# Seven block products in the order 1 5 6 2 7 3 4, with sums chained through PSUM pairs that ScalarE starts, and the last round's preparation one round later

## Chip, core and metric

One Trainium2 chip, one of its cores (core 0). The metric is the device time of one execution in microseconds. Before the change three runs took 802.03, 802.43 and 801.37 us, median 802.03.

The engines named below are TensorE (PE, with PEld for its weight loads), VectorE (DVE), ScalarE (ACT), GpSimd (POOL) and SyncE (SP). POOL and SP do almost nothing here but issue transfers: SP the loads, POOL the stores and the transfers that add to what lies at their target.

## The reference, cut to what matters

With x of 2048 rows (S) and 512 columns (D), weights of F = 1792 columns, all in fp32:

```python
# A: Fourier mixing, real part
a = x @ dft_hid_re.T
b = x @ dft_hid_im.T
A = dft_seq_re @ a - dft_seq_im @ b
# B: gated feed-forward
gate, up = x @ W_gate, x @ W_up
B = (gate * (gate > 0) * up) @ W_down
# mix, one gate value per row of x
g = sigmoid((x * gate_w).sum(-1, keepdims=True))
out = g * A + (1 - g) * B
```

## The kernel before

**Arithmetic.** Every fp32 operand is split into a high part and a low rest (a cast on ScalarE, then a subtraction on VectorE), and every product is three matmuls: high by low, low by high, high by high (`PARTS`, line 375). The large products are cut into 2 x 2 blocks and done with seven block products instead of eight. Which blocks are added to form the operands of product m stands in `LEFT` and `RIGHT` (lines 25 to 28); the tables are for the block stages, the rounds have their own sums in `Left.sum` (729) and `Sequence.rights` (874). Each matmul is 128 x 128 stationary by 512 columns moving, so a result is one PSUM bank (128 partitions x 512 fp32). There are eight banks. A `Pair` (339) is two banks.

**Stages in TensorE's order** (the letters are the names of the PSUM tiles in the profile):

- `c`: eight warm-up matmuls, then `Direct` (544, 96 matmuls, plain products for the first weight columns), then eleven `Block`s (491) of 84 matmuls. A Block is one (c, q): 256 columns of the gate and of the up weights by one half of the rows, as seven products of 12 matmuls, 6 into each bank of a pair (gate in one, up in the other). Weights of a new c are loaded and split by `w_prep` (458) while the block before runs.
- `a`: four `SpectralBlock`s (655), 84 matmuls each, for a and b.
- `c` again: two Blocks.
- `z`: two `Down` rounds (843, h @ W_down, 294 matmuls each) and four rounds with the sequence matrices, three `Sequence` (865) and the `Last` (904), 336 matmuls each. A round is seven products of 48 matmuls, in the order `ORDER_Z` (710). The left operands of the last two rounds were split earlier, stored, and are fetched back during the second of the four rounds (`Left.fetch`, 759, tensor `lb`).

**After a product.** The evacuations read the finished banks and combine them. In a Block (`evac`, 515) they work on one bank at a time: ScalarE copies or rectifies 512 wide, VectorE adds 512 wide from a bank and from SBUF (`t`, `u`). The sums that several products share are kept in SBUF. In a round (`Round.evac`, 811) `both` does the same bank by bank.

**PSUM.** A pool of eight tiles of one bank, handed out in turn; the first matmul into a bank overwrites (`start=True`). A Block takes six banks and the next one the two that are left, then those that are free again.

**The mix.** In the third and fourth rounds results are multiplied by the gate row and added to what earlier rounds stored in DRAM (`vd`, `zd`). For the Last round `prepare` (907) loads both, multiplies, adds and stores the sum back in `vd`, four pieces of 512 KB each from each of the two: eight loads, four stores, eight VectorE instructions 1024 wide. It is given `start + 150`, where start is the key at which the second round begins.

**Who sets the order.** Nothing is left to a scheduler of the language. Each step gets a key in units of one matmul (`op`), and `Plan` (129) lays out, once, when the program is built, an order for each engine, from a key, a due time and its own table of durations (`Step`, 90; `order`, 196). SBUF is 51 units of 4 KB per partition (`UNITS`); a step that begins a new buffer waits in the plan until a unit is free. On the chip each engine then runs its list in order, and waits where it must.

Lines that the change and the steps of the prediction touch: `ORDER`, `BANK` 29 and 30; `run` 262; `Weights` 414 and `w_prep` 458; `Block.evac` 515; `Spectral.prep` 646 and `SpectralBlock.evac` 680; `ORDER_Z` 710; `Round` 766, `evac` 811; `Sequence.rights` 874; `Last` 904 to 946; the keys from 960 to 1072.

Of the kernel before, what the change touches and what calls it, by code (L numbers as in the profile page):

```python
# [14 lines left out]
P = 128  # L15
# [9 lines left out]
LEFT = {1: ("11", "22", 1), 2: ("21", "22", 1), 3: ("11",), 4: ("22",), 5: ("11", "12", 1),  # L25
        6: ("21", "11", -1), 7: ("12", "22", -1)}
RIGHT = {1: ("11", "22", 1), 2: ("11",), 3: ("12", "22", -1), 4: ("21", "11", -1), 5: ("22",),
         6: ("11", "12", 1), 7: ("21", "22", 1)}
ORDER = (5, 2, 1, 3, 4, 6, 7)
BANK = {5: "a", 3: "a", 6: "a", 2: "b", 4: "b", 7: "b", 1: "c"}  # L30
# [98 lines left out]
class Plan:  # L129
# [30 lines left out]
    def read(self):  # L160
# [3 lines left out]
        seen, banks = {}, []  # L164
        for s in self.steps:
            for refs, writes in ((s.reads, False), (s.writes, True)):
                for r in refs:
# [7 lines left out]
                    if not r.base.uses and r.base.kind == "bank":  # L175
                        banks.append(r.base)
                    r.base.uses.append(s)

        for old, new in zip(banks, banks[8:]):
            new.uses[0].after.update(x for x in old.uses if x is not new.uses[0])  # L180
# [81 lines left out]
    def run(self, nc, unit, bank):  # L262
# [5 lines left out]
        for b in self.bufs:  # L268
            if b.uses and b.kind in ("unit", "bank"):
                first.setdefault(min(at[s] for s in b.uses), []).append(b)  # L270

        held, idle = [-1] * UNITS, [-9.0] * UNITS
        for n, s in enumerate(self.steps):
            for b in first.get(n, ()):
                if b.kind == "bank":
                    b.tile = bank(b)
                    continue
# [9 lines left out]
def kernel(ctx: ExitStack, tc, xP, xG, wf, wgu, wd, cr, ci, wri, gw, out):  # L287
# [19 lines left out]
    psum = ctx.enter_context(tc.tile_pool(name="psum", bufs=8, space=PSUM))  # L307
# [28 lines left out]
    def bank(b):  # L336
        return psum.tile([P, N], F32, name=b.name, tag="ps")

    class Pair:


        def __init__(self, name):
            self.name, self.banks = name, None

        def new(self):
            self.banks = [Buf(plan, self.name, [N], kind="bank") for _ in range(2)]

        def __getitem__(self, n):
            return self.banks[n].all
# [37 lines left out]
    def x_raw(q, m):  # L387

        a, *r = RIGHT[m]
        raw = piece[q, {6: "12", 7: "21"}[m] if m in (6, 7) else a] if not r or m in (6, 7) else buf(f"xs{m}")  # L390
        X[q, m] = buf(f"xh{m}", dtype=F32R), buf(f"xl{m}", dtype=F32R), raw

    def x_sum(q, m):
        a, *r = RIGHT[m]
        if r:
            combine(X[q, m][2].all, piece[q, a].all, piece[q, r[0]].all, r[1])
# [15 lines left out]
    SLOT = {5: 0, 1: 1, 2: 2, 4: 0, 3: 1, 7: 2, 6: 3}  # L412

    class Weights:
        def __init__(self, c):
            self.c = c
            self.raw = [buf(f"wr{i}", [4, 2, P]) for i in range(2)]
            self.sum = [buf(f"ws{i}", [3, 2, P]) for i in range(2)]
# [6 lines left out]
        def a_sum(self, i):  # L425
            r, o = self.raw[i], self.sum[i]
            E().vector.tensor_add(o[:, 0], r[:, 1], r[:, 2])
            E().vector.tensor_add(o[:, 1], r[:, 0], r[:, 1])
            E().vector.tensor_add(o[:, 2], r[:, 0], r[:, 3])
            E().scalar.copy(self.a[i][0].all, o.all)  # L430

        def a_lo(self, i):
            E().vector.tensor_sub(self.a[i][1].all, self.sum[i].all, f32(self.a[i][0].all))

        def b_sum(self, i):
            r = self.raw[i]
            E().vector.tensor_sub(r[:, 2:4], r[:, 2:4], r[:, 0:2])

        def b_hi(self, i):
            E().scalar.copy(self.b[i][0].all, self.raw[i].all)  # L440

        def b_lo(self, i):
            E().vector.tensor_sub(self.b[i][1].all, self.raw[i].all, f32(self.b[i][0].all))
# [11 lines left out]
        def of(self, m, i):  # L455
            return [t[:, SLOT[m]] for t in (self.a if m in (5, 1, 2) else self.b)[i]]
# [34 lines left out]
    class Block:  # L491


        def __init__(self, q, w):
            self.q, self.w = q, w
            self.t, self.g, self.u = buf("t"), buf("g"), buf("u")
            self.h = [buf(f"h{d}") for d in range(2)]
            self.ps = {k: Pair("c") for k in "abc"}
            for m in ORDER:
                for i in range(2):  # L500
                    pe(6, self.product, m, i)
                    self.evac(m, i, plan.now)
            h_out(q, w.c, self.h, plan.now + (8 if plan.now > 270 else 100))

        def product(self, m, i):
            w, x, ps = self.w.of(m, i), X[self.q, m], self.ps[BANK[m]]
            if m in (5, 2, 1) and i == 0:
                ps.new()
            n = 0
            for k in range(2):  # L510
                for a, b in PARTS:
                    mm(ps[i], w[a][:, k], x[b][:, k], start=m in (5, 2, 1) and n == 0, stop=n == 5)
                    n += 1

        def evac(self, m, i, key):
            a, b, c = (self.ps[k] for k in "abc")
            t, g, h = self.t, self.g, self.h

            def go():
                e = E()  # L520
                if m == 5:
                    e.scalar.copy(t[:, i], a[i])
                elif m == 2:
                    e.vector.tensor_add(t[:, i], t[:, i], b[i])
                elif m == 1:
                    e.vector.tensor_sub(t[:, i], c[i], t[:, i])

                elif m in (3, 4):
                    j, ps = (0, a) if m == 3 else (1, b)
                    if i == 0:  # L530
                        e.scalar.activation(g[:, j], ps[0], AF.Relu)
# [234 lines left out]
    class Round:  # L766
# [25 lines left out]
        def product(self, x, jj):  # L792
# [3 lines left out]
            if first:  # L796
                ps.new()
# [330 lines left out]
```

## Time and profile before

| what | value |
|---|---|
| median of three runs | 802.03 us (801.37 to 802.43) |
| span of the profiled execution, first to last instruction | 799.7 us |
| PE busy | 790.3 us, 99% of the span, 3464 matmuls |
| DVE busy | 665.6 us, 83% |
| ACT busy | 329.1 us, 41% |
| POOL busy | 91.7 us, 11% |
| moved by DMA | 192.79 MB, mean 241 GB/s |
| granted TensorE clock, mean | 0.999 |

The profile gives no device time of its own for the profiled execution; its span stands 2.3 us under the median, which is what lies around the span. All steps carry line 126, since a helper of the plan issues them; groups are told apart by the names of the tiles. `c`, `a` and `z` are PSUM tiles, `ch`/`cl` the high and low parts of a right operand of a round, `r` a loaded piece of a sequence matrix (from `cr` or `ci`), `lb` the stored left operands, `wr` raw weights, `ws` their sums. Matmuls are pipelined: each row lasts 0.39 us, and one starts about every 0.227 us.

### The profile page before, as it was taken

The numbers are of one execution on the slowest core, as the hardware profiler recorded it, in microseconds if no ns is written. First come the engines' busy times: TensorE is split into PE (matmuls) and PEld (weight loads), VectorE is DVE, ScalarE is ACT, GpSimd is POOL, SyncE is SP. The second block draws the span as 40 slices with busy tenths as digits, with TensorE's granted clock in tenths as the row PEclk, the third lists the DMA queues.
The fourth block names the chain that finished last, engine by engine and source line by source line (L and its number), as shares of the span: only waits on it lengthen the run. The fifth ranks groups of instructions, "written<-read, shape, count | busy, mean of one in ns | idle before, by whom it ended". The sixth has DMA issues, their size and how long they took to land.

```text
span 799.7 us, 9573 instructions
## 1 busy us (share of the span) xinstructions
PE 790.3 (99%) x3464; PEld 652.1 (82%) x3464; DVE 665.6 (83%) x791; ACT 329.1 (41%) x393; POOL 91.7 (11%) x146
## 2 busy tenths in 40 slices
PE   8999999999999999999999999999999999999997
PEld 7888888888888888888888888888888877888885
DVE  7999977868699466999985799996688849988995
ACT  5533221212133144275665668454334335434530
POOL 0101211111112122111131011001000100010000
PEclk9999999999999999999999999999999999999999
DMA  9514553232547599999899989118899995197424
GB/s 346 219 41 145 183 200 145 92 145 93 197 145 250 198 353 400 416 343 344 291 373 413 409 278 370 72 58 244 267 333 401 344 384 178 40 305 270 153 64 143
DMA packets 55039, 192.79 MB, mean 241 GB/s; under 512 B 6352, under 2 KB 6352, under 8 KB 54992
## 3 DMA queue, kind: packets, MB, share of 16 engines
q1 hardware_dynamic: 35120, 120.87, 41.6%
q0 software_dynamic: 19296, 70.26, 25.2%
q10 hardware_dynamic: 576, 1.05, 0.4%
q8 instruction: 27, 0.44, 0.2%
q14 instruction: 20, 0.16, 0.1%
HBM read 120.85 MB, written 71.31 MB: 240 GB/s over the span
## 4 chain that ended last, share of the span: by engine, by line
PE 91%; DMA 6%; DVE 2%; ACT 0%; issue 0%; SPq 0%; ACTq 0%; DVEq 0%
PE z L126 48%; PE c L126 34%; PE a L126 10%; DMA r<-ci 4%; DMA lb<-lb 1%; DVE cl L126 1%; DMA wf<-wf 1%; DVE r L126 0%; ACT ch L126 0%; DVE v L126 0%; DVE z L126 0%; ACT wf0h L126 0%; SPq L126 0%; ACTq L126 0%; DVEq L126 0%
## 5 line engine op out<-in xcount | busy, mean ns | idle before, releaser
L126 ACT CAST ch<-r 128x1024 fp32r<-128x1024 f32 x112 | 116.1, 1053 | 140.8 <-DVE r L126 54.6
L126 PE MATMUL z<-ch,ll 128*128 128x512 f32 x420 | 163.4, 389 | 0.0
L126 PE MATMUL z<-cl,lh 128*128 128x512 f32 x420 | 163.4, 389 | 0.0
L126 PE MATMUL z<-ch,lh 128*128 128x512 f32 x420 | 163.4, 389 | 0.0
L126 DVE TENSOR_TENSOR cl<-r,ch 128x1024 fp32r<-128x1024 f32 x112 | 134.6, 1221 | 27.4 <-ACT ch L126 20.5
L126 PE MATMUL z<-ch,lb 128*128 128x512 f32 x448 | 138.4, 389 | 0.7 <-ACT ch L126 0.7
L126 PEld LDWEIGHTS z<-ch,lb 128*128 128x128 f32 x448 | 84.1, 188 | 18.4 <-ACT ch L126 1.1
L126 PEld LDWEIGHTS z<-ch,lh 128*128 128x128 f32 x420 | 78.8, 188 | 16.5
L126 PEld LDWEIGHTS z<-ch,ll 128*128 128x128 f32 x420 | 78.8, 188 | 16.3
L126 PEld LDWEIGHTS z<-cl,lh 128*128 128x128 f32 x420 | 78.8, 188 | 16.3
L126 PE MATMUL z<-cl,lb 128*128 128x512 f32 x224 | 87.5, 391 | 1.4 <-DVE cl L126 1.3
L126 DVE TENSOR_TENSOR r<-r,r 128x1024 f32<-128x1024 f32 x64 | 76.5, 1219 | 3.6 <-DMA r<-ci 3.0
L126 DVE TENSOR_TENSOR cl<-hr,ch 128x1024 fp32r<-128x1024 f32 (+1 forms) x56 | 59.9, 1087 | 13.4 <-ACT ch L126 10.8
L126 ACT CAST ch<-hr 128x1024 fp32r<-128x1024 f32 (+1 forms) x56 | 51.3, 941 | 28.4 <-DMA hr<-hd 13.8
L126 PEld LDWEIGHTS z<-cl,lb 128*128 128x128 f32 x224 | 42.0, 188 | 11.3 <-DVE cl L126 2.6
L126 ACT ACTIVATE g<-c 128x512 f32<-128x512 f32 x26 | 15.5, 598 | 66.4 <-PE c L126 66.2
L126 PE MATMUL c<-xh,wb0l 128*128 128x512 f32 x104 | 40.5, 389 | 0.0
L126 PE MATMUL c<-xl,wb0h 128*128 128x512 f32 x104 | 40.5, 389 | 0.0
L126 PE MATMUL c<-xh,wb0h 128*128 128x512 f32 x104 | 40.5, 389 | 0.0
L126 PE MATMUL c<-xh,wb1l 128*128 128x512 f32 x104 | 40.5, 389 | 0.0
L126 PE MATMUL c<-xl,wb1h 128*128 128x512 f32 x104 | 40.5, 389 | 0.0
L126 PE MATMUL c<-xh,wb1h 128*128 128x512 f32 x104 | 40.5, 389 | 0.0
(191 smaller groups left out, 1321.3 us busy)
## 6 DMA issues: line engine op xcount, KB each, us to landing
hr<-hd SPq DMA_DIRECT2D x42, 512.0 KB, 7.4
r<-cr SPq DMA_DIRECT2D x32, 512.0 KB, 5.6
r<-ci SPq DMA_DIRECT2D x32, 512.0 KB, 9.2
hd<-hs POOLq DMA_DIRECT2D x28, 512.0 KB, 4.7
lb<-lb SPq DMA_DIRECT2D x28, 512.0 KB, 12.0
ad<-a POOLq DMA_DIRECT2D x16, 512.0 KB, 6.0
l<-ad SPq DMA_DIRECT2D x16, 512.0 KB, 8.8
wr<-wgu SPq DMA_DIRECT2D x14, 512.0 KB, 5.5
```

Source lines behind the costliest of these rows:

```text
L126: getattr(getattr(nc, self.engine), self.name)(*map(ap, self.a), **{k: ap(x) for k, x in self.k.items()})
```

## The change

- **Products.** All seven-product stages use one scheme in the order 1 5 6 2 7 3 4 (rounds: 1 5 6 3 7 2 4). `LEFT` and `RIGHT` give new operands; some are sums of a sum (product 6 of the right operand is block 22 minus the operand of 5). An x stage has four sums instead of five, and product 3 of the first half of the rows shares its split with `Direct`.
- **PSUM.** One tile of eight banks for the whole kernel, as four fixed pairs x, m, y, t. Only products 1 and 5 begin with `start=True`. ScalarE starts the others: after product 1 it copies pair x to pair y, and 6 and 7 accumulate there; after product 7 it copies y, negated, to t, and 4 accumulates there; 2 goes on in x and 3 in m. Pairs y and t are thus begun by ScalarE's write.
- **Evacuations** take both banks in one instruction, 1024 wide. In a Block ScalarE has four of 1024 and two of 512 (before: four of 512), VectorE two of 1024 and four of 512 (before: twelve of 512). In a round before the Last, ScalarE has six of 1024 (before: six of 512), VectorE two of 1024 (before: eight of 512 and one of 1024).
- **Weights.** The parts used by 1, 2, 4 need no sums; those for 5, 6, 7, 3 have four sums 256 wide, and are all prepared ahead of the block that uses them.
- **Keys.** `prepare` at `start + 540` with 40 between the pieces (before: `start + 150`, 24); refetch of the weights of c = 1 begins 140 ahead (before: 90); the `Last` round has no `ahead` step any more.

The diff, cut to its core:

```diff
-LEFT = {1: ("11", "22", 1), 2: ("21", "22", 1), 3: ("11",), 4: ("22",), 5: ("11", "12", 1),
-        6: ("21", "11", -1), 7: ("12", "22", -1)}
...
-ORDER = (5, 2, 1, 3, 4, 6, 7)
-BANK = {5: "a", 3: "a", 6: "a", 2: "b", 4: "b", 7: "b", 1: "c"}
+LEFT = {1: ("11",), 2: ("12",), 3: ("12", 6, -1), 4: ("22",), 5: ("21", "22", 1), 6: (5, "11", -1), 7: ("11", "21", -1)}
+RIGHT = {1: ("11",), 2: ("21",), 3: ("22",), 4: (6, "21", -1), 5: ("12", "11", -1), 6: ("22", 5, -1), 7: ("22", "12", -1)}
+ORDER = (1, 5, 6, 2, 7, 3, 4)
+BANK = {1: "x", 2: "x", 5: "m", 3: "m", 6: "y", 7: "y", 4: "t"}
+FIRST = (1, 5)
...
-    psum = ctx.enter_context(tc.tile_pool(name="psum", bufs=8, space=PSUM))
+    psum = ctx.enter_context(tc.tile_pool(name="psum", bufs=1, space=PSUM))
...
+    ps8 = Buf(plan, "ps", [8, N], kind="fixed", tile=psum.tile([P, 8, N], F32, name="ps"))
...
+    PAIRS = {k: Pair(n) for n, k in enumerate("xmyt")}
...
     def w_prep(w, key, ahead=66):
         for i in range(2):
             op(key - ahead + 6 * i, w.load, i)
-            op(key - 36 + 12 * i, w.a_sum, i)
+            op(key - 36 + 12 * i, w.a_hi, i)
             op(key - 30 + 12 * i, w.a_lo, i)
-            op(key + 6 * i, w.b_sum, i)
-            op(key + 6 * i, w.b_hi, i)
-        op(key + 6, w.b_lo, 0)
-        op(key + 12, w.b_lo, 1)
+            op(key - 40 + 12 * i, w.b_sum, i)
+            op(key - 34 + 12 * i, w.b_hi, i)
+            op(key - 26 + 12 * i, w.b_lo, i)
...
+        def evac(self, m, key):
+            x, y, p, t = (PAIRS[k] for k in "xymt")
+            e = E()
+
+            def rectified(r, j, ps, sign):
+                g, h = self.g[r], self.h[int(r[0]) - 1][:, j]
+                op(key, lambda: e.scalar.activation(g.all, ps[0], AF.Relu, scale=sign))
+                if sign > 0:
+                    op(key + 1, lambda: e.vector.tensor_mul(h, g.all, ps[1]))
                 else:
...
+                    op(key + 1, lambda: e.vector.scalar_tensor_tensor(h, ps[1], sign, g.all, op0=OP.mult, op1=OP.mult))
+
+            def added(r, ps, s):
+                u, h = self.u[r], self.h[int(r[0]) - 1][:, 1]
+                op(key, lambda: e.vector.tensor_add(u.all, ps.all, s.all))
+                op(key + 1, lambda: e.vector.scalar_tensor_tensor(h, u[:, 0], 0.0, u[:, 1], op0=OP.max, op1=OP.mult))
+
+            if m == 1:
+                op(key, lambda: e.scalar.copy(y.all, x.all))
+            elif m in (5, 6):
+                op(key, lambda: e.scalar.copy(self.s[m].all, (p if m == 5 else y).all))
+            elif m == 2:
+                rectified("11", 0, x, 1.0)
+            elif m == 7:
+                op(key, lambda: e.scalar.activation(t.all, y.all, AF.Copy, scale=-1.0))
+                added("22", y, self.s[5])
+            elif m == 3:
+                added("12", p, self.s[6])
+            elif m == 4:
+                rectified("21", 0, t, -1.0)
...
-    ORDER_Z = (1, 3, 5, 7, 6, 2, 4)
+    ORDER_Z = (1, 5, 6, 3, 7, 2, 4)
...
             if x == 1:
-                op(key, lambda: both(E().scalar.copy, self.u, a))
-            elif x == 5:
-                op(key, lambda: both(E().scalar.copy, self.n5, b))
-            elif x == 6:
-                op(key, lambda: both(E().vector.tensor_sub, self.w, b, self.u))
-                op(key + 1, lambda: both(E().vector.tensor_add, o["12"], e, self.w))
+                op(key, lambda: e.scalar.activation(Y, X, AF.Copy, scale=-1.0))
+            elif x in (5, 6):
+                op(key, lambda: e.scalar.copy(s[x].all, M if x == 5 else Y))
+            elif x == 3:
+                op(key, lambda: e.vector.tensor_add(o["12"].all, M, s[6].all))
                 self.done("12", key + 6)
-                op(key + 14, lambda: both(E().vector.tensor_add, o["22"], d, self.w))
-                self.done("22", key + 20)
-                op(key + 34, lambda: E().vector.tensor_sub(self.u2.all, self.w.all, self.n5.all))
+            elif x == 7:
+                op(key, lambda: e.scalar.copy(T, Y))
+                op(key + 8, lambda: e.vector.tensor_add(o["22"].all, Y, s[5].all))
+                self.done("22", key + 14)
...
-                for b, key in (("11", at[1, jj]), ("22", at[3, jj]), ("12", at[5, jj]), ("21", at[2, jj] - 36)):
+                for b, key in (("11", at[1, jj]), ("12", at[5, jj]), ("22", at[6, jj] - 10), ("21", at[2, jj] - 36)):
...
-                k, z, v = key + 24 * i, buf("z"), buf("v")
+                k, z, v = key + 40 * i, buf("z"), buf("v")
...
-            def ahead():
-                E().vector.tensor_mul(self.u2.all, self.u2.all, self.gate("21"))
-                combine(v.all, v.all, self.u2.all, -1)
             op(key - 90, lambda: load(v.all, vd[self.place("21")]))
-            op(key - 40, ahead)
...
-        for m, k in ((3, -90), (5, 10), (7, 48), (6, 88), (2, 130), (4, 170)):
+        for m, k in ((5, -90), (6, 10), (3, 48), (7, 88), (2, 130), (4, 170)):
...
-            Last(lefts[m], m, p).prepare(start + 150)
-
-    plan.run(nc, unit, bank)
+            Last(lefts[m], m, p).prepare(start + 540)
+
+    plan.run(nc, unit)
```

`SpectralBlock.evac` is changed like `Block.evac`, with the results written straight to the output tiles.

More of the change, by code (lines that the diff above doesn't have):

```diff
@@ L260, in order, with run @@
         self.steps = sorted(done, key=lambda s: s.start)
-    def run(self, nc, unit, bank):
+    def run(self, nc, unit):
         self.read()
@@ L417, in __init__ @@
             self.raw = [buf(f"wr{i}", [4, 2, P]) for i in range(2)]
-            self.sum = [buf(f"ws{i}", [3, 2, P]) for i in range(2)]
+            self.sum = [buf(f"ws{i}", [4, 2, P]) for i in range(2)]
             self.a = [[buf(f"wa{i}{x}", [3, 2, P], F32R) for x in "hl"] for i in range(2)]
@@ L572, in products @@
                 first = d == k == n == 0
-                if first and i == 0:
-                    self.ps[f, j].new()
                 a, b = PARTS[2 - n]
@@ L793, in product @@
             c = self.c[x, jj]
-            ps = self.ps[{1: "A", 3: "E", 5: "B", 7: "D", 6: "B", 2: "A", 4: "D"}[x]]
-            first, last = x in (1, 3, 5, 7) and jj == 0, jj == len(self.counts) - 1
-            if first:
-                ps.new()
+            ps = PAIRS[BANK[x]]
+            first, last = x in FIRST and jj == 0, jj == len(self.counts) - 1
             for d in range(2):
```

204 lines of the change are left out of this document (78 added, 126 removed).

## The prediction

> **What bounds the kernel now.** I read the engine table of the page first, then the chain of work that ended last, the timeline around its ends, and the stretches of 20 us.
>
> ```profile
> span 799.7 us, 9573 instructions
> PE 790.3 (99%) x3464; PEld 652.1 (82%) x3464; DVE 665.6 (83%) x791; ACT 329.1 (41%) x393; POOL 91.7 (11%) x146
> ```
>
> ```profile
> 5.85 233.22 PE c L126 x1020
> 239.07 76.16 PE a L126 x336
> ...
> 353.31 255.69 PE z L126 x1128
> ...
> 614.94 11.94 DMA lb<-lb
> ...
> 626.95 17.55 DMA r<-ci
> ...
> 644.56 12.54 DMA r<-ci
> ...
> 666.61 126.56 PE z L126 x557
> 793.17 0.02 issue
> ```
>
> ```profile
> 18.59 0.39 PE L126 MATMUL c<-xb12h,wf0h 128*128 128x512 f32 x1
> ```
>
> ```profile
> 794.12 0.39 PE L126 MATMUL z<-ch,lb 128*128 128x512 f32 x1
> 794.55 0.69 DVE L126 TENSOR_TENSOR z<-z,gg 128x512 f32<-128x512 f32 x1
> ...
> 795.27 0.69 DVE L126 TENSOR_TENSOR v<-v,z 128x512 f32<-128x512 f32 x1
> ```
>
> TensorE is the bound, and its pace is in the `a` row: 76.16 / 336 = 0.22667 us a matmul. Eight of the 3464 are warm-up; 3456 need 783.4 us. They begin at 5.85, and the last starts at 794.12 and gives up its slot at 794.35: 788.5 us, so 5.1 us are lost in between. Where? Product by product: the 49th starts at 18.59, 12.74 us after the first, where 48 slots are 10.88: 1.86 us are lost while the first pieces land and are split. From there to 609 nothing is: the first two PE rows and the `z` row of 1128 run at the pace to within the 0.16 us by which a row outlasts its slot. The chain then leaves PE until 666.61, and 5.1 - 1.86 leaves a hole of about 3.2 us there. The matmul counts of the stretches agree:
>
> ```profile
> 420.00:440.00 20.00, 20.00 (x90) 16.55 (x89) 11.84 (x12) 10.46 (x13) 2.18 (x5) 1.00 1.03 413
> ...
> 600.00:620.00 20.00, 20.00 (x90) 16.57 (x89) 17.07 (x16) 8.66 (x9) 1.11 (x3) 1.00 1.01 402
> 620.00:640.00 20.00, 20.00 (x90) 16.57 (x89) 15.93 (x17) 6.29 (x8) 3.08 (x4) 1.00 1.04 342
> 640.00:660.00 20.00, 18.53 (x81) 14.79 (x80) 9.07 (x9) 7.01 (x8) 0.84 (x1) 1.00 1.03 384
> 660.00:680.00 20.00, 19.36 (x85) 15.38 (x84) 19.65 (x18) 10.58 (x11) 0.00 (x0) 1.00 0.49 173
> 680.00:700.00 20.00, 20.00 (x90) 16.57 (x89) 19.86 (x20) 9.82 (x10) 0.85 (x1) 1.00 0.14 45
> ```
>
> Columns are PE, PEld, DVE, ACT, POOL busy (with counts), clock, DMA share, GB/s. 640 to 680 has 81 + 85 matmuls where 90 + 90 are the rule: 14 too few, 14 x 0.22667 = 3.2 us. I take 3.1. DMA is full from 600 to 660, `r<-ci` took 12.5 and 17.6 us to land, and VectorE, starved in 640 to 660 (9.07 of 20 us), then ran after the lost time. So the hole is late loads.
>
> What can be won is therefore 3.1 us: the start (1.86) is not touched, nor is the tail, where the two pairs of VectorE instructions on the last product and the store stay as they are.
>
> **The change, part by part.**
>
> *Preparation moved.* The second round spans 562.8 to 639.0, the third 639.0 to 717.5.
>
> ```profile
> 562.80:639.00 76.20, 76.20 (x338) 63.08 (x337) 62.13 (x58) 28.52 (x31) 5.59 (x8) 1.00 0.97 339
> 639.00:717.50 78.50, 76.39 (x333) 62.06 (x332) 64.07 (x60) 34.11 (x36) 3.38 (x4) 1.00 0.66 222
> ```
>
> ```profile
> lb<-lb SPq DMA_DIRECT2D x28, 512.0 KB, 12.0
> ...
> z<-zd SPq DMA_DIRECT2D x4, 512.0 KB, 9.0
> vd<-v POOLq DMA_DIRECT2D x4, 512.0 KB, 7.4
> ```
>
> ```profile
> 589.98 0.36 SPq L126 DMA_DIRECT2D z<-zd  x1
> ```
>
> ```profile
> 619.98 0.53 POOL L126 DMA_DIRECT2D vd<-v  x1 [9.19 <-DVE v L126]
> ```
>
> The preparation is 4 loads of z, 4 of v and 4 stores, 12 x 0.524 MB = 6.3 MB; at the 413 GB/s of a full stretch (420 to 440), 15.2 us of DMA. They were issued between about 590 and 620, ahead in the queue of the loads that came late, and beside the 28 fetches of `lb`. Without them the second round's share falls from 0.97 to 0.97 - 15.2/76.2 = 0.77, and the late loads get up to 15 us back where 3.1 were missing. The step is worth -3.1, all of the hole. Its key is now 540 matmuls after 562.8, which is 685; loads begin 50 matmuls earlier, and the fourth piece starts 27 us later. The third round, 0.66 of 78.5 us, becomes at most (51.8 + 15.2)/75.4 = 0.89, and part of its 51.8 (the backlog of 639 to 660) goes forward into the second. Its stretch 660 to 700 is nearly free (0.49, 0.14). SP's queue is passed by 8 issues, POOL's by 4 stores; the stores wait for VectorE, and behind them wait the `z<-zd` accumulations, which feed results, not TensorE. VectorE gets 8 more instructions there: see below.
>
> *Evacuations.* Prices:
>
> ```profile
> L126 DVE TENSOR_TENSOR u<-c,t 128x512 f32<-128x512 f32 x26 | 17.9, 687 | 2.6 <-PE c L126 2.4
> ...
> L126 ACT ACTIVATE g<-c 128x512 f32<-128x512 f32 x26 | 15.5, 598 | 66.4 <-PE c L126 66.2
> ...
> L126 ACT COPY t<-c 128x512 f32<-128x512 f32 x26 | 15.3, 588 | 59.5 <-PE c L126 59.5
> ...
> L126 ACT ACTIVATE n<-z 128x1024 f32<-128x1024 f32 x8 | 8.4, 1058 | 2.7 <-DVE z L126 2.7
> ...
> L126 DVE TENSOR_TENSOR u<-w,n 128x1024 f32<-128x1024 f32 x6 | 7.3, 1220 | 1.9 <-DMA vd<-z 1.9
> ```
>
> A Block: VectorE 12 x 0.687 = 8.2 becomes 4 x 0.687 + 2 x 1.22 = 5.2, so -3.0; ScalarE 4 x 0.59 = 2.4 becomes 2 x 0.6 + 4 x 1.06 = 5.4, +3.1. A round: VectorE 8 x 0.687 + 1.22 = 6.7 becomes 2.4; ScalarE 3.5 becomes 6.4. Over 13 Blocks, 4 SpectralBlocks and 6 rounds some 75 us leave VectorE. Neither engine is the bound, so on the path this is 0. In the third round VectorE has 64.1 + 8 x 1.22 - 4.3 = 69.6 of 75.4 us.
>
> *The new waits.* TensorE now waits for ScalarE between products: 6 for the copy of x to y, 7 for the copy of y out, 4 for the copy into t. Behind the waiting matmul all others queue. In a round one product (48 matmuls, 10.9 us) lies between, and in a Down round 9.5: covered. In a Block and a SpectralBlock only 12 matmuls, 2.72 us. A copy can start 0.18 after the slot ends (0.16 of pipeline, 0.02 issue), so with 1.06 it is ready at 1.24 of 2.72. No row here shows a copy of 1024 from PSUM, nor one into it. Bounds: one row of 1024 (1.06), and twice that (2.12); I take 1.06, since 512 from a bank cost 0.59, no more than half of 1024. (The Trainium skill, "ScalarE: Activation LUTs", in "Step-by-step: what each stage is for", says ScalarE writes faster to PSUM than to SBUF; by that the copy would be cheaper still, and the sum unchanged. No row shows it.) Other ScalarE work can stand ahead:
>
> ```profile
> 153.43 0.60 ACT L126 ACTIVATE g<-c 128x512 f32<-128x512 f32 x1 [6.21 <-PE c L126]
> 153.93 0.82 ACT L126 CAST wa0h<-ws 128x768 fp32r<-128x768 f32 x1
> 154.65 1.05 ACT L126 CAST wb0h<-wr 128x1024 fp32r<-128x1024 f32 x1
> ...
> 158.91 1.05 ACT L126 CAST wb1h<-wr 128x1024 fp32r<-128x1024 f32 x1 [0.58 <-DVE wr L126]
> ```
>
> With one cast of 1.05 ahead the copy ends at 2.29: covered by 0.43. ScalarE's list is laid out by start times, so two casts ahead are not expected. Value 0; the other end is in the second rival.
>
> ```profile
> L126 DVE TENSOR_TENSOR ws<-wr 128x256 f32<-128x256 f32 x42 | 15.3, 419 | 0.0
> ...
> L126 DVE TENSOR_TENSOR wr<-wr 128x512 f32<-128x512 f32 x14 | 9.5, 686 | 0.1
> ```
>
> *Weights and x.* Sums for 5, 6, 7, 3 move ahead of the block: four 256 wide (15.3/42 = 0.36 each) replace three and one of 512, 0.3 us less per half of a weight load; and one x sum less per half of the rows. If the b parts could only begin when product 3 of the block before ends, 24 matmuls (5.44 us) remain to product 5; hi, lo of both halves need about 2 x 1.05 + 2 x 1.22 = 4.5. Covered, value 0.
>
> *Tail.* The two `ahead` instructions had run by 787.5, before the end: 0.
>
> ```profile
> 786.26 1.23 DVE L126 TENSOR_TENSOR v<-v,u 128x1024 f32<-128x1024 f32 x1
> ```
>
> Sum: 799.7 - 3.1 = 796.6 us span; with the 2.3 by which the median stands above the span, 798.9. I add 0.1 for a copy that is late here or there: **799.0 us**, own range 798.3 to 800.2.
>
> **Rivals.**
>
> *First: the late loads move with the preparation.* The third and fourth round take 12 more transfers and 9.8 us of VectorE. For: 0.89 as the upper bound of the third round's share, and VectorE at 69.6 of 75.4, with 680 to 700 at 19.86 of 20 already. Against: that 19.86 is the catch-up after the hole, and of the 14.4 us in which VectorE stood idle in the third round 10.9 are in 640 to 660, the wait that goes. If the same hole opens 80 us later, 799.0 + 3.1 = 802.1. The same time results if it was the 28 `lb` fetches alone that filled the queue, and moving the rest does not empty it.
>
> *Second, on the other side: the handoff through PSUM is late in the 12-matmul products.* Place: the wait of product 4 for t, after 7. There two engines read y, the copy to t (1.06) and VectorE's add (1.22). If they take turns with VectorE first, behind a cast of 1.05 on ScalarE: 0.18 + 1.05 + 1.22 + 1.06 = 3.51, 0.79 after the 2.72. It can occur in the six Blocks before which weights are split, and in the four SpectralBlocks, where ScalarE also splits operands: ten handoffs x 0.79 = 7.9, 806.9. It decides from six late handoffs (4.7 us, 803.7). Against: it needs both the cast and the order at once. (The Trainium skill speaks for it: "PSUM — Partial Sum Buffer", in "Terms", says that two engines on one bank at once are an error, "reads against reads included", so the two readers must take turns. By that alone, without the cast, the copy ends at 2.46 and the sum stays. No row of before has two engines on one bank.) A copy of 2.12 into PSUM behind a cast gives 3.35, 0.63 late, and leads to nearly the same time.
>
> **How the numbers follow.** The first forecast has 0.60; the first rival 0.18; the second 0.17; 0.05 stays for smaller losses of both kinds. A measurement of this kernel tells about 0.2%, 1.6 us, from no change: faster is below 800.4, slower above 803.6. Faster: 0.60 + 0.01 = 0.61. Same: the first rival and some of the rest, 0.19. Slower: 0.20, the second rival and the first where its hole is doubled. The range reaches from 798.3 (a hole of 3.2 and runs that differ by half a us) to 804.5, which takes in the first rival and the second up to seven late handoffs; what lies above is 0.12, below 0.04.
>
> **What would show it.** Right: 640 to 680 with 90 matmuls per 20 us, the chain on PE without a break from 19 to 794 less 3, DMA share in 600 to 660 well below 1, DVE near 585 us and ACT near 400. First rival: PE idle before `r` or `cl` between 690 and 760 and DMA at 1.0 there. Second: PE waits for ACT with outputs in PSUM, 0.1 to 0.8 us each, between 30 and 353, at products 6, 7 or 4; the copies would last over 1.1 us or start late behind a cast. The forecast is wrong if PE busy loses more than 1.5 us anywhere that it did not lose before.

## The result, and the profile after

| | before | after |
|---|---|---|
| median | 801.70 us (799.53 to 802.43, 4 runs) | 808.34 us (807.16 to 809.14, 4 runs) |
| ratio after / before | | 1.0091, 95% interval 1.0073 to 1.0109 |
| span of the profiled execution | 799.7 us | 807.3 us (its device time 809.14) |

The change makes the kernel slower by some 0.9%. The forecast was 799.0 with 804.5 as the top of the range, so direction and range are both wrong. (Here and below a ratio comes with its interval; the quotient of the two medians may differ from it, here 1.0083, but lies inside the interval each time.)

All steps now carry line 125, and all of PSUM is one tile, `ps`. The copy of pair x to pair y is `ACT COPY ps<-ps`, the negated copy into t is `ACT ACTIVATE ps<-ps`. The page of the changed kernel begins with the span and the engines' busy times:

```profile
span 807.3 us, 9404 instructions
PE 792.6 (98%) x3464; PEld 652.1 (81%) x3464; DVE 588.1 (73%) x643; ACT 387.4 (48%) x418; POOL 92.0 (11%) x146
```

VectorE lost 77.5 us and ScalarE gained 58.3, but the time went up. TensorE's waits say where: the view of waits for PE alone (waited for, us in total, times, longest) shows

```profile
PE ps L125 <- DVE cl L125: 4.9, 4, 2.5
PE ps L125 <- ACT ps L125: 2.4, 1, 2.4
PE ps L125 <- DVE gs L125: 1.5, 1, 1.5
PE ps L125 <- ACT wf0h L125: 0.5, 1, 0.5
PE ps L125 <- ACT s L125: 0.3, 1, 0.3
```

The third and fourth are at the start, which the kernel before had too. New are four waits for `cl`, VectorE's low part of a right operand in a round, and one long wait for ScalarE's write into PSUM. The stretches of 20 us say when (columns as in the prediction: PE, PEld, DVE, ACT, POOL, clock, DMA share, GB/s):

```profile
300.00:320.00 20.00, 17.39 (x76) 13.71 (x75) 9.93 (x9) 12.39 (x14) 7.57 (x13) 1.00 1.03 418
...
640.00:660.00 20.00, 20.00 (x90) 16.58 (x89) 12.53 (x11) 8.14 (x8) 0.84 (x1) 1.00 0.89 324
660.00:680.00 20.00, 20.00 (x90) 16.57 (x89) 14.50 (x13) 8.04 (x8) 0.00 (x0) 1.00 0.46 144
680.00:700.00 20.00, 20.00 (x90) 16.54 (x90) 16.49 (x14) 7.27 (x7) 1.42 (x2) 1.00 0.72 223
700.00:720.00 20.00, 17.98 (x78) 14.26 (x77) 15.53 (x14) 9.74 (x10) 2.82 (x4) 1.00 0.86 268
720.00:740.00 20.00, 17.50 (x76) 13.52 (x75) 16.10 (x15) 6.15 (x6) 1.43 (x2) 1.00 1.03 359
740.00:760.00 20.00, 19.60 (x85) 15.59 (x84) 20.00 (x18) 9.97 (x10) 0.00 (x0) 1.00 0.55 187
```

The old hole is gone: 640 to 680 has its 90 + 90 matmuls. A new one stands at 700 to 760 with 78, 76 and 85, and another at 300 to 320 with 76. To size them I took the starts of all matmuls in the timeline and counted, for each pair of neighbours, what exceeds the pace of 0.22667 us:

| where | before | after |
|---|---|---|
| start (to about 11 us) | 1.7 | 2.35 |
| fourth SpectralBlock, 307 to 316 | 0 | 0.41 + 2.51 = 2.9 |
| old hole, 652 to 667 | 0.87 + 1.03 + 0.28 + 0.69 = 2.9 | 0 |
| third to fourth round, 710 to 756 | 0 | 0.83 + 1.52 + 0.18 + 2.65 + 0.17 + 0.56 = 5.9 |
| sum | 4.6 | 11.2 |

That is +6.6 of the 7.6 us between the spans. Most of the other 1.0 is in gaps below 0.12 us: the second matmul behind such a gap comes 0.11 late too (nine times after, three before), and over the Blocks small gaps add up to 0.2. The start needs no cause in the change: it lost between almost nothing and 2.2 us in the profiles of the kernels below, and most of these change nothing before the last rounds. There the matmuls stand 0.43 us apart for some us without a wait between them (the last section has the same pace), so two profiles can differ by 2 us for this alone. So there are two things to explain, 5.9 us and 2.9 us. (Below, sizes of waits of TensorE are excesses of this kind, some 0.16 us more than the idle time in the row, unless a row is read.)

**What ends the waits after 700.** First the matmul behind the longest, from PE's timeline of the changed kernel (start, duration, and in brackets the idle time before and who ended it), then VectorE's timeline of the same stretch:

```profile
738.48 0.50 PE L125 MATMUL ps<-cl,lb 128*128 128x512 f32 x1 [2.48 <-DVE cl L125]
```

```profile
714.78 1.23 DVE L125 TENSOR_TENSOR cl<-r,ch 128x1024 fp32r<-128x1024 f32 x1 [2.01 <-DMA vd<-v]
...
737.20 1.23 DVE L125 TENSOR_TENSOR cl<-r,ch 128x1024 fp32r<-128x1024 f32 x1 [2.39 <-DMA out<-z]
```

These two `cl`, for which TensorE waits 1.36 us at 716.06 and 2.48 at 738.48, stood for a *store*, which has nothing to do with their inputs. A subtraction that reads `r` and `ch` can wait for `vd<-v` or `out<-z` only because its output goes into the SBUF unit which the store still reads. `vd<-v` is the preparation's own store, of which there are four. `out<-z` isn't: it puts a finished result of the third round into the output, before the change too. The chain of waits has it at its full length:

```profile
722.21 14.90 DMA out<-z
...
737.20 0.10 DVE cl L125
```

The store of 512 KB was under way for 14.9 us, in a stretch where the DMA engines were at 1.03. The first of the four waits, 0.66 us at 711.69, goes back to the preparation as well. ScalarE stood for another of its stores:

```profile
700.47 1.05 ACT L125 CAST ch<-r 128x1024 fp32r<-128x1024 f32 x1 [5.13 <-DMA vd<-v]
```

Behind this cast stood its copy of y into t (701.43), for that copy VectorE waited 4.32 us until 702.47, and from there VectorE ran without a pause up to the `cl` of 710.42, which came late.

**What ends the wait at 313.** PE's row, then ScalarE's timeline:

```profile
316.11 0.50 PE L125 MATMUL ps<-vh,xl 128*128 128x512 f32 x1 [2.35 <-ACT ps L125]
```

```profile
306.94 1.02 ACT L125 COPY s<-ps 128x1024 f32<-128x1024 f32 x1 [1.49 <-DMA lb<-lh]
311.60 1.01 ACT L125 COPY a<-ps 128x1024 f32<-128x1024 f32 x1 [3.64 <-DMA lb<-ll]
314.10 1.04 ACT L125 CAST lh<-lr 128x1024 fp32r<-128x1024 f32 x1 [1.49 <-DMA lb<-lh]
315.05 1.01 ACT L125 ACTIVATE ps<-ps 128x1024 f32<-128x1024 f32 x1
```

The row at 315.05 is the copy into t that product 4 needs. It waits for nobody itself; it stands in ScalarE's list behind an evacuation and a cast, and these waited 3.64 and 1.49 us for the stores `lb<-ll` and `lb<-lh` to give up units. The smaller loss of 0.41 us at 307 is the copy out at 306.94, late for the same reason. The DMA issues of the changed kernel (KB each, median us from issue to landing):

```profile
lb<-lb SPq DMA_DIRECT2D x28, 512.0 KB, 5.4
...
lb<-lh POOLq DMA_DIRECT2D x14, 512.0 KB, 10.2
lb<-ll POOLq DMA_DIRECT2D x14, 512.0 KB, 11.2
...
vd<-v POOLq DMA_DIRECT2D x4, 512.0 KB, 8.3
```

The fetches `lb<-lb`, which took 12.0 us before, now take 5.4: the relief of the second round is real. The stores take 8 to 11 from their issue, where the plan that fixed every engine's list counts 2.1 us after a transfer's turn in the queue (`LANDING`).

**The prices.** The groups by shape (busy time, mean ns):

```profile
L125 ACT COPY s<-ps 128x1024 f32<-128x1024 f32 x42 | 42.6, 1015 | 56.9 <-PE ps L125 54.5 <-DMA lb<-lh 1.5 <-ACT xh L125 0.8
L125 ACT ACTIVATE ps<-ps 128x1024 f32<-128x1024 f32 x23 | 23.2, 1008 | 41.4 <-DVE u L125 23.2 <-PE ps L125 15.2 <-DVE a L125 2.9
L125 ACT COPY ps<-ps 128x1024 f32<-128x1024 f32 x23 | 23.0, 999 | 60.5 <-PE ps L125 40.8 <-DVE z L125 19.7
```

A copy into PSUM takes 1.00 us, out of it 1.015: a little under the lower bound of 1.06 that the prediction took.

### The profile page after: what moved, and what is told of

Same layout as the page of the kernel before. It is cut to its first block, busy times and chain, and to the rows that moved or that the text cites. A ratio compares the mean times of both kernels' runs of the same rounds, so it can differ in the third digit from the quotient of the medians.

```text
span 807.3 us, 9404 instructions
## 1 busy us (share of the span) xinstructions
PE 792.6 (98%) x3464; PEld 652.1 (81%) x3464; DVE 588.1 (73%) x643; ACT 387.4 (48%) x418; POOL 92.0 (11%) x146
## 5 line engine op out<-in xcount | busy, mean ns | idle before, releaser
L125 PE MATMUL ps<-ch,ll 128*128 128x512 f32 x420 | 163.4, 389 | 0.0
L125 PE MATMUL ps<-cl,lh 128*128 128x512 f32 x420 | 163.4, 389 | 0.0
L125 PE MATMUL ps<-ch,lh 128*128 128x512 f32 x420 | 163.4, 389 | 0.0
L125 PE MATMUL ps<-ch,lb 128*128 128x512 f32 x448 | 138.2, 389 | 0.0
L125 PEld LDWEIGHTS ps<-ch,lb 128*128 128x128 f32 x448 | 84.1, 188 | 17.3
L125 PE MATMUL ps<-cl,lb 128*128 128x512 f32 x224 | 88.0, 393 | 4.9 <-DVE cl L125 4.9
L125 PEld LDWEIGHTS ps<-cl,lh 128*128 128x128 f32 x420 | 78.9, 188 | 16.5
L125 PEld LDWEIGHTS ps<-ch,lh 128*128 128x128 f32 x420 | 78.9, 188 | 16.3
L125 PEld LDWEIGHTS ps<-ch,ll 128*128 128x128 f32 x420 | 78.9, 188 | 16.2
L125 ACT COPY s<-ps 128x1024 f32<-128x1024 f32 x42 | 42.6, 1015 | 56.9 <-PE ps L125 54.5
```

Source lines behind the costliest of these rows:

```text
L125: getattr(getattr(nc, self.engine), self.name)(*map(ap, self.a), **{k: ap(x) for k, x in self.k.items()})
```

## The experiments

Two readings of the trace are weighed in them, and the expectations put numbers to both. By the one, the *place* of the preparation decides: its transfers and VectorE instructions are too much for the third round's end. By the other it is the *order*: each engine runs a list fixed when the program is built, and the list puts an instruction whose unit a late store still holds ahead of one that TensorE needs; then moving nothing and only planning with later landings should help as well. Each ratio is to runs of the kernel before that were made beside it; their medians were 801.2, 800.83 and 801.0.

### Is it the preparation's place?

**The preparation put back** in the changed kernel.

```diff
-                k, z, v = key + 40 * i, buf("z"), buf("v")
+                k, z, v = key + 24 * i, buf("z"), buf("v")
...
-            Last(lefts[m], m, p).prepare(start + 540)
+            Last(lefts[m], m, p).prepare(start + 150)
```

> The changed kernel with the preparation of the Last round put back to where it was (start + 150, 24 apart). Theory 1 (the moved preparation opened the waits of TensorE between 710 and 756, 5.9 us): those waits go, and the old hole between 650 and 667 (2.9 us) opens again or not; 802.5 to 805.5 us. Rival (the new product order and the 1024-wide evacuations of the rounds opened them): the waits stay between 710 and 756 and the old hole adds to them; 808 to 811 us. Under both, the wait of product 4 for ScalarE's copy near 313 us stays, 2.5 us.

Measured: 804.18 us, ratio 1.0056 (1.0036 to 1.0076). No wait is left after 700, and the old hole is back, 1.24 + 1.06 = 2.3 us at 655 to 658:

```profile
640.00:660.00 20.00, 18.14 (x80) 14.45 (x79) 10.81 (x10) 8.04 (x8) 0.84 (x1) 1.00 1.03 387
660.00:680.00 20.00, 20.00 (x90) 16.57 (x89) 18.79 (x18) 11.21 (x12) 0.00 (x0) 1.00 0.56 212
...
700.00:720.00 20.00, 20.00 (x90) 16.57 (x89) 12.94 (x12) 7.29 (x8) 1.70 (x2) 1.00 0.91 286
720.00:740.00 20.00, 20.00 (x90) 16.53 (x89) 19.98 (x18) 11.10 (x11) 0.85 (x1) 1.00 0.74 256
```

So the moved preparation causes the 5.9 us, and does remove the hole. The wait near 313 stays (2.54), so it is another matter.

**Only the move**, in the kernel before.

```diff
-                k, z, v = key + 24 * i, buf("z"), buf("v")
+                k, z, v = key + 40 * i, buf("z"), buf("v")
...
-            Last(lefts[m], m, p).prepare(start + 150)
+            Last(lefts[m], m, p).prepare(start + 540)
```

> The kernel before with nothing changed but the preparation, at start + 540 and 40 apart. Theory 1: the hole between 650 and 667 goes (-2.9) and new waits for cl open between 705 and 760 (+4 to +8); 803 to 807 us. Rival: no new waits, 799 us.

Measured: 800.95 us, ratio 1.0006 (0.9996 to 1.0016): no difference, as the first rival foretold. The hole at 640 to 680 is gone, and 4.6 us are lost at 716 to 728: waits of 0.48 and 2.53, and 1.6 in slow matmuls behind them (last section):

```profile
640.00:660.00 20.00, 20.00 (x90) 16.53 (x90) 11.60 (x11) 7.51 (x9) 0.84 (x1) 1.00 0.87 317
...
720.00:740.00 20.00, 17.63 (x71) 14.25 (x71) 17.74 (x18) 9.18 (x10) 1.44 (x2) 0.91 0.95 349
```

The rival's reason holds in part. What was late is a load, but not of `r`: VectorE stood for a piece that the third round's own mix adds, and the `cl` that TensorE needed stood two places behind in its list.

```profile
718.98 1.22 DVE L126 TENSOR_TENSOR z<-z,v 128x1024 f32<-128x1024 f32 x1 [1.91 <-DMA v<-vd]
```

The move alone is no gain in the old kernel, and none of what the change does to products or PSUM is needed for its loss. The expectation had the time too high, 803 to 807. Part of the even result is luck: this profile loses 0.8 at the start, where the kernel before loses 1.7.

**The preparation left out** of the changed kernel (so the Last round adds to what the rounds before had stored, without the products with the gate row).

```diff
-            Last(lefts[m], m, p).prepare(start + 540)
+            Last(lefts[m], m, p)
```

> The changed kernel without the preparation: no loads of z and v for it, no multiply and add, no store; the gated sum of the first sequence round is left out of the output. Theory 1: the waits between 710 and 756 go, and none takes their place; 802 to 803 us, what is left above 799 being the wait near 313. Rival: they stay, 807 to 809.

Measured: 802.34 us, ratio 1.0010 (0.9994 to 1.0027). No wait after 700, none at 640 to 680. What is left is the wait near 313, 2.73 us, and slow matmuls behind it, 1.5 (last section). So even with the preparation for nothing, the change gains nothing: its other parts have a loss of their own that is no smaller than the hole.

### Which part of the preparation?

**Without its VectorE instructions**: transfers alone.

```diff
-                op(k, lambda b=b, z=z: E().vector.tensor_mul(z.all, z.all, self.gate(b, g)))
-                op(k + 2, lambda v=v, z=z: combine(v.all, v.all, z.all, 1))
```

> The changed kernel with the eight transfers in and four out of the preparation, but without its eight VectorE instructions (the multiply and the add are left out of the output). If the transfers and the SBUF units that they hold make the waits: 806 to 808 us, waits between 710 and 756 at 4 us or more. If VectorE's 9.8 us make them: they go, 802 to 803.5.

Measured: 805.45 us, ratio 1.0065 (1.0049 to 1.0082). One wait of 2.47 us at 722, with slow matmuls of 1.5 behind it, together 4.0 against 5.9. The result lies between the two expectations: transfers alone are enough for most of the loss. That VectorE's eight instructions make it longer isn't shown, since the intervals of the two kernels overlap. Here it is a load that VectorE stood for:

```profile
722.30 1.22 DVE L125 TENSOR_TENSOR r<-r,r 128x1024 f32<-128x1024 f32 x1 [7.16 <-DMA r<-ci]
```

This load took 15.9 us. A store has its part in it: by the chain of waits SP, which issues the loads, stood for a `vd<-v` of 11.6 us until 698.56, and the loads of `r` are behind that in its list.

**Without its four stores**: loads and VectorE instructions stay, the sum isn't put back.

```diff
-                op(k + 10, lambda b=b, v=v: store(vd[self.place(b)], v.all))
```

> The changed kernel with the preparation at its new place, its eight loads and eight VectorE instructions, but without its four stores (the gated sum of the first sequence round is left out of the output). If the four stores and the units that they hold until they land are the main cost: waits after 700 under 2 us, 803 to 804.5 us, the wait near 313 remaining. If the loads and VectorE's work are: 4 us or more after 700, 806 to 808.

Measured: 801.88 us, ratio 1.0004 (0.9983 to 1.0025), below the 803 to 804.5 expected; its four runs lie at 799.4, 800.0, 803.8 and 803.8. The wait near 313 remains, 2.44 us and 1.6 behind it. No wait after 700, with all of the preparation's VectorE instructions in place:

```profile
700.00:720.00 20.00, 20.00 (x90) 16.53 (x90) 19.42 (x17) 8.29 (x8) 1.71 (x2) 1.00 0.97 312
720.00:740.00 20.00, 20.00 (x90) 16.57 (x89) 17.76 (x16) 8.25 (x8) 0.84 (x1) 1.00 0.87 324
```

The DMA engines are still at 0.97 and 0.87, and VectorE is busier at 700 to 720 than in the kernel that waits (19.42 against 15.53). So neither a full DMA nor a full VectorE is enough for the hole; it takes the stores. The run takes away their traffic and the units they hold at one stroke, and doesn't part these two. That the traffic counts shows on the other store: `out<-z`, 14.9 us in the changed kernel, took 11.0 here.

**Earlier in the third round**, spacing unchanged. (The recorded expectation says that the pieces are 24 apart; in the kernel that ran they are 40 apart, as in the change.)

```diff
-            Last(lefts[m], m, p).prepare(start + 540)
+            Last(lefts[m], m, p).prepare(start + 430)
```

> The changed kernel with the preparation between the two places, start + 430 and 24 apart. Theory 1: the waits that it opens come earlier and where DMA and SBUF units are freer (660 to 700), so that those after 700 shrink to under 3 us; 803 to 806 us. If they stay at 5 or more the place inside the third round does not matter.

Measured: 801.71 us, ratio 1.0005 (0.9991 to 1.0018), below the 803 to 806 expected. Every stretch from 640 to 760 has 90 matmuls: neither the old hole nor the new one. The third round can take the preparation; 110 matmuls (25 us) decide. The wait near 313 stays, 2.72 us and 1.7 behind it.

**The same thought in the kernel before**: the preparation in the third round, 24 apart.

```diff
-            Last(lefts[m], m, p).prepare(start + 150)
+            Last(lefts[m], m, p).prepare(start + 480)
```

> The kernel before with the preparation alone moved, to start + 480, 24 apart. The old hole (2.9 us) goes; if fewer transfers of the preparation meet those of the end of the third round than at 540 and 40, the waits after 705 are under 2 us; 798.5 to 800.5 us. If not, 801 as with 540.

Measured: 798.83 us, ratio 0.9985 (0.9973 to 0.9997), 2.0 us by the medians and 1.2 by the ratio. So a move of the preparation can win in the kernel before, at another key: 1.2 to 2.0 of the 3.1 us that the prediction put on it, though at 0.15% it is less than a measurement was taken to tell. Two waits under 1 us remain (0.92 at 423, 0.96 at 684).

### The wait of product 4 near 313

**VectorE writes t** in the SpectralBlocks, so that ScalarE's list no longer lies on the handoff.

```diff
-                e.scalar.activation(t, y, AF.Copy, scale=-1.0)
+                e.vector.tensor_scalar(t, y, -1.0, None, op0=OP.mult)
```

> The changed kernel with one instruction of each SpectralBlock moved: the negated copy of y into t, for which product 4 waits, is made by VectorE instead of ScalarE. Theory 2 for the first wait (the copy stands behind casts on ScalarE that wait for a store of lb to land): the wait near 313 goes or falls under 0.7 us; 805 to 806.5 us. Rival (the copy itself, from and to PSUM, is what is late): it stays at 2 us or more, 808 to 809.

Measured: 806.61 us, ratio 1.0077 (1.0052 to 1.0102), just above the 805 to 806.5 expected. The wait near 313 is gone: VectorE (first fence) writes t at 312.44, while ScalarE (second fence) still stood for a store until 312.36:

```profile
312.44 1.23 DVE L125 TENSOR_SCALAR ps<-ps 128x1024 f32<-128x1024 f32 x1
```

```profile
312.36 1.02 ACT L125 COPY a<-ps 128x1024 f32<-128x1024 f32 x1 [3.71 <-DMA lb<-ll]
```

But VectorE's list has the same kind of trouble: a new wait of 1.90 us at 292 to 294, ended by VectorE's write into PSUM (the instructions ahead of it stood for a cast, and the cast for a load, `l<-ad`), and one of 0.90 at 308 for ScalarE's copy out. After 700 it still loses 6.0, of which 1.5 are slow matmuls. Which engine writes t matters less than what stands ahead of it.

**The plan counts later landings**, nothing else is touched. Of the program that runs, the order of the lists differs, and which unit a buffer gets, since `run` takes for it the unit that by the plan has been free longest.

```diff
-    MATMUL, WAIT, LANDING = 0.22667, 0.035, 2.1
+    MATMUL, WAIT, LANDING = 0.22667, 0.035, 5.0
```

> The changed kernel with one constant of the plan changed: a transfer is planned to land 5.0 us after its share of the queue instead of 2.1. The work is the same; the lists of the engines differ. Theory 2 (the waits come from engines that stand, in their fixed order, behind an instruction whose SBUF unit is freed by a transfer that lands later than planned): the wait of product 4 near 313 us falls from 2.5 to under 1, the waits between 710 and 756 from 5.9 to under 3; 800 to 804 us. Rival (a resource is simply full there, DMA or VectorE): both stay, 807 to 809.

Measured: 799.40 us, ratio 0.9987 (0.9972 to 1.0001). By the two ratios (1.0091 and 0.9987) that is 1.0%, some 8 us, below the changed kernel, with the same steps. Near 313 the wait has gone, and ScalarE's timeline shows why:

```profile
308.86 1.01 ACT L125 ACTIVATE ps<-ps 128x1024 f32<-128x1024 f32 x1 [0.98 <-PE ps L125]
312.33 1.05 ACT L125 CAST lh<-lr 128x1024 fp32r<-128x1024 f32 x1 [2.47 <-DVE lr L125]
```

The copy into t now stands ahead of the cast, and waited only for TensorE. After 700, 1.22 + 0.61 us are left of the 5.9, with the preparation at `start + 540`:

```profile
720.00:740.00 20.00, 18.95 (x84) 15.38 (x83) 17.90 (x17) 9.81 (x10) 0.00 (x0) 1.00 0.81 298
740.00:760.00 20.00, 19.55 (x86) 15.87 (x86) 19.96 (x18) 11.46 (x13) 0.00 (x0) 1.00 0.49 167
```

The stores are no faster here: the four `vd<-v` take 6.6 to 10.4 us, and the `out<-z` of 14.9 takes 15.8, but VectorE and ScalarE stand for none of them after 695. Two new waits of 0.54 and 0.27 us open at 335 and 340. So both losses come from what stands in the lists behind late transfers. Near 313 the rows show that it is the order; after 700 order and choice of units changed together, and no run parts them. The preparation's place counts because it brings four more stores, and makes others later.

**The plan counts later landings for POOL's transfers alone** (the stores), then **with the preparation at 430** too.

```diff
-                s.end = line + self.LANDING + (2.0 if "accum_op" in s.k else 0)
+                s.end = line + self.LANDING + (2.0 if "accum_op" in s.k else 0) + (2.9 if s.engine == "gpsimd" else 0)
```

```diff
-            Last(lefts[m], m, p).prepare(start + 540)
+            Last(lefts[m], m, p).prepare(start + 430)
```

> The changed kernel with the plan's landing lengthened by 2.9 us for the transfers that POOL issues (stores and accumulations) and left at 2.1 for loads. If it is the SBUF units held by stores that block the engines' lists: the wait near 313 falls under 1 us and the waits after 700 under 3; 800 to 803 us. If late loads matter more, the waits after 700 stay at 4 or more and only the one near 313 goes; 804 to 806.

> The changed kernel with that longer landing of stores and the preparation at start + 430, 40 apart. The parts that cost time are both undone: no wait near 313, none after 700, and the old hole between 650 and 667 does not come back; 796.5 to 798.5 us, faster than both kernels. If one of the two cures spoils the other, 800 or more.

Measured: 801.29 us, ratio 1.0010 (0.9998 to 1.0021), for the first; 799.17 us (798.27 to 799.97), ratio 0.9976 (0.9967 to 0.9985), for both. The first cures the wait near 313 and leaves 0.37 + 1.02 + 0.61 us after 700. The 1.02 stand behind an `out<-z` of 16.3 us, a store that SP issues and that this edit doesn't touch. With both, every stretch that had a hole runs at the pace, to within one matmul:

```profile
300.00:320.00 20.00, 20.00 (x89) 16.23 (x88) 11.07 (x10) 11.95 (x14) 5.46 (x10) 1.00 1.03 418
...
700.00:720.00 20.00, 20.00 (x90) 16.57 (x89) 15.13 (x14) 7.94 (x8) 1.70 (x2) 1.00 1.03 313
720.00:740.00 20.00, 20.00 (x90) 16.53 (x90) 19.80 (x18) 10.15 (x11) 0.00 (x0) 1.00 0.57 199
```

DMA is at 1.03 in two of these stretches, and no matmul waits. This version beats both kernels, the one before by 1.8 us by the medians. It is 0.7 us above the top of what was expected of it; two waits of 0.62 and 0.54 us for ScalarE's write into PSUM remain, at 291 and 331. That the new products and pairs are worth anything isn't shown by this: the kernel before with nothing but the preparation moved stands at 798.83, and no run gives the kernel before the longer landing.

## Why the prediction was wrong

- **What bounds the kernel** (TensorE, and a hole of 3.1 us that is late loads in the second round): right. The hole, 2.9 by the starts and 3.3 with the small gaps behind, went when the preparation went, in every kernel here that has the preparation later or not at all, and came back with it. The 1.86 us at the start were misread, which costs the sum nothing: no matmul waits there for pieces that land; they run 0.43 us apart.
- **"The step is worth -3.1, all of the hole"**: here the prediction failed. The gain was right; the cost at the new place was taken as nothing, and was 5.9: 2.3 at the end of the third round, 3.6 in the fourth, which begins at 721.4 and for which no DMA share was worked out. I argued with a share of DMA averaged over the round, at most 0.89, and with VectorE's sum. After the change the four stretches from 640 to 720 average 0.73, under that bound, while 720 to 740 stands at 1.03: the mean said nothing of the place where the transfers meet. And a share isn't what stops TensorE: without the four stores DMA stood at 0.97 without a wait. What I had to ask was which instruction is next in VectorE's list, or in ScalarE's, when a store still holds the unit that this instruction writes to.
- **"the stores wait for VectorE, and behind them wait the `z<-zd` accumulations, which feed results, not TensorE"**: I followed what is behind the stores in POOL's queue, and not what is behind them in SBUF. `cl` at 714.78 waited 2.01 us for `vd<-v`, and TensorE for `cl`; the cast at 700.47 waited 5.13.
- **The first rival** (the late loads move with the preparation, 802.1) had the place and the sign, PE idle for `cl` between 690 and 760 and DMA at 1.0 there, and was priced by the old hole, 3.1 instead of 5.9. For the move alone in the old kernel its time was good, no change, but by the starts 4.6 are lost there for 2.9 won, and the start makes up the rest. Why the same move costs 5.9 in the new kernel is open; the two kernels' lists differ in all of the round.
- **"two casts ahead are not expected. Value 0"**: the second step that failed, by 2.9 us. The copy into t was late once in 17 handoffs of 12 matmuls (13 Blocks, 4 SpectralBlocks), not for its price or for engines that take turns, as the second rival had it, but because two instructions ahead of it in the list stood for stores. The prediction counted instructions ahead by their durations; it had no term for an instruction ahead that itself waits.
- **Handoffs in the Blocks, value 0**: right; in the changed kernel none of the thirteen Blocks has a gap over 0.12 us after the start. The two readers of y do take turns, VectorE first, as its row in one Block (first fence) and ScalarE's (second) show:

```profile
138.95 1.23 DVE L125 TENSOR_TENSOR u<-ps,s 128x1024 f32<-128x1024 f32 x1 [1.96 <-PE ps L125]
```

```profile
140.21 1.01 ACT L125 ACTIVATE ps<-ps 128x1024 f32<-128x1024 f32 x1 [4.74 <-DVE u L125]
```

  The copy began when VectorE had read y and still ended in time. With that the trace agrees with the rule from the Trainium skill that the prediction cited ("PSUM — Partial Sum Buffer"), and with its sum: 0.
- **Evacuations, weights, tail, value 0**: nothing in the profile of the changed kernel speaks against it. VectorE came to 588.1 (585 foretold), ScalarE to 387.4 (400), the copies to 1.00 us (1.06). Those 77 us of VectorE's time bought nothing, as was said.
- **The sum**: the span foretold was 796.6; add 5.9, 2.9, 0.2 for the hole's size, 0.6 at the start and the 1.0 in small gaps: 807.2, where 807.3 was measured. (It has to close, since the terms are read from the two profiles.) The 2.3 us from span to device time were too much: in every run with both numbers it is 1.7 to 1.9.
- **The chances**: 0.12 was left above the range. Both late waits were among the rivals by place, but each alone; that both hold at once had no case of its own.

What stays open is how much of the 5.9 is the stores' traffic and how much the units they hold. The kernel without stores removes both. The kernel with only the plan's landing changed keeps both and loses 1.8 instead of 5.9, which speaks for order and units; that one `out<-z` is 3.9 us shorter without the four stores speaks for a share of the traffic.

## What to carry to other kernels

Where every engine runs a list fixed in advance, an instruction waits for its output's buffer as well as for its inputs, and all that is behind it waits too: when transfers move, look for the stores that hold buffers near the new place, and for what the lists have behind the instruction that takes such a buffer. A list is as good as the landings it was laid out with; here planning with 5.0 us instead of 2.1 after a transfer's turn, where stores took 8 to 11 from their issue, was worth some 8 us of the changed kernel. A DMA share averaged over 75 us can't say that a place in it is free.

## What the runs showed of the hardware

A wait of TensorE of some 2.4 us can cost more than itself. In the kernel with the preparation put back, PE waited 2.38 us before 313.95, and 1.3 us later its matmuls started 0.43 us apart instead of 0.227. Its PE timeline, and then the stretch of 5 us:

```profile
314.98 0.48 PE L125 MATMUL ps<-vl,xh 128*128 128x512 f32 x1
315.26 0.63 PE L125 MATMUL ps<-vh,xh 128*128 128x512 f32 x1
315.69 0.63 PE L125 MATMUL ps<-vh,xl 128*128 128x512 f32 x1
```

```profile
315.00:320.00 5.00, 5.00 (x16) 3.95 (x15) 4.70 (x5) 2.96 (x4) 1.54 (x3) 0.66 1.03 414
```

The clock granted is 0.66 over this stretch; PE counts as busy throughout, with 16 matmuls where 22 fit. It lasted about 3.3 us (315.0 to 318.3) and cost 1.6. Six other profiled kernels show the like behind a wait of 1.9 to 2.6 us; in the one with 1.9, where VectorE writes t, the clock is 0.66 from 737 to 742. In the profile of the changed kernel the waits of 2.35 and 2.48 us did not bring it, with the clock at 1.00 in the stretches above, nor did one of 2.7 us in the kernel without the preparation's VectorE instructions. The first matmuls of most of these kernels are 0.43 us apart too, with no wait between them. In the kernel before, four that begin at 7.69 us take until 9.40:

```profile
7.69 1.91 PE L126 MATMUL c<-xb11l,wf0h 128*128 128x512 f32 x4
```

There the clock in the view reads 1.00 (5 to 15 us), so the spacing of the matmuls is the safer sign.

The Trainium skill, "TensorE: Matmul & The Clock Gate", in "Part 1: The HAM clock gate (the "warmup" mystery)", has a gate that passes half of the clock after an idle window of about 3.4 us, with windows that run on by themselves whatever the kernel does. The half rate agrees with 0.43 against 0.227, the length with 3.3 us, and windows of that kind would let the same wait bring it in one run and not in the next. But here waits shorter than a window were enough.
